# Hedgehog attention and squared-ReLU FFN: k's first tiles through the hardware queues, v's scaling in column pairs, q by whole rows

## Chip, cores and metric

The kernel runs on one core of a Trainium2 chip. The metric is the device time of one execution in microseconds; 11 executions of the kernel before were timed. A profiled execution has its own time, and a trace whose span begins with the first and ends with the last instruction.

## What is computed

```
phi(x)  = concat(exp(p), exp(-p)),  p = x @ w_phi - max|x @ w_phi|   # per row
kv      = phi(k)^T @ v              # per head: 256 x 64
z       = sum over rows of phi(k)
attn    = (phi(q) @ kv) / (phi(q) @ z + 1e-6)
x       = attn, heads side by side  # 4608 x 512
out     = relu(x @ w_in)^2 @ w_out  # 512 -> 2048 -> 512
```

q, k and v are 8 batches of 8 heads of 576 rows of 64, w_phi is 64 x 128, all fp32; the output is 4608 x 512, fp32. On chip the operands of all matmuls are bf16.

## The kernel before, in words

**Tiles.** A batch has 576 rows: 512 of each head go through tiles of 128 rows x 4, two heads (a pair) at a time, and the last 64 of each head, the short rows ("s", tile group 4), through tiles in which two heads lie one below the other. The FFN works on chunks of 512 rows: chunk c is the 512 long rows of batch c, and the ninth chunk holds the short rows of all batches (`xS`). The 8 batches' attention and the 9 chunks' FFN are interleaved, so that TensorE works on the FFN of one batch while VectorE and ScalarE prepare the next.

**A batch's attention.** k and q are loaded, transposed (`kT`, `qT`; on TensorE at line 616 for batches 0 and 1, by a transposing DMA on SP at line 626 for the others) and multiplied with w_phi (L642; for batch 0's k L670, for its q L816; q once more in the other orientation at L858). VectorE takes the maximum of the absolute values along a row (`mk` L722 and L677, `mq` L823). ScalarE takes exp of both signs (`kp`, `kn` L728 and L705; `qp`, `qn` L873). The maximum of k isn't subtracted ahead of exp: ScalarE turns it into the factors exp(-m) and exp(m) (L747; short rows L740), which stand in the 65th column of `va`, and VectorE multiplies v with them into the other 64 (L766; short rows L762). TensorE forms kv and z in one matmul of 65 columns (L783, L788), a copy brings it to `kv_sb`, and TensorE multiplies it with `qp` and `qn` (L888). VectorE scales the first part by `en` (L900), takes the reciprocal of the 65th column (L908) and multiplies (L912), which gives `xo`. Transposed (`xT`; L928 and L937 for batch 0, else by DMA), this is the FFN's input.

**A chunk's FFN.** 16 blocks of w_in (L1038; for chunk 0 in smaller pieces L1049), relu into `hr` on ScalarE or VectorE (L1015, L1017), the square into `h` on VectorE (L1024), w_out (L1103; the last tile L1067), a copy to `ot` (L441 or L439) and a store by SP.

**What sets the order.** Every step is entered in a plan as an operation with an engine, a cost, a key and what it reads and writes. A planner (`Machine.run`) runs through it with these costs, with the eight PSUM banks and with a model of the DMA queues, and writes the instructions of every engine in the order in which it picked them; `KEYS` are the sort keys of all operations, `RELEASES` are the earliest times of loads, and `STATES` tells for the operations that two engines can do (a plan's `either`) which one takes it. All of this is fixed when the kernel is built. Each engine then works through its list in order and waits by semaphores.

**Loads.** All loads but w_phi are issued by POOL (software queue), which casts fp32 to bf16 under way: per batch k and v in runs of 512-element pairs (`load`, L512), q in two halves of the columns of each row group (`load_q`, L532: 128 of 256 fp32 values of a row, 512 B), the short rows in two DMAs (L520). The first k pair is issued on its own. w_phi comes by the hardware queues of SP and ACT, a half each (L476). At most 8 software DMAs are under way: the ninth waits for the first.

**Fillers.** Where the plan has TensorE idle in the first 45 us, and a PSUM bank is free (`op.spare`), matmuls on a zero tile `warm` are inserted (L1195): at a cost of 0.11 us each up to 6 us, of 0.058 us after.

The scaling of v, before:

```
o = t[:, 8 * g0 : 8 * g1, :]
pin(nc.vector.tensor_tensor(
    out=o[:, :, :D], in0=xv[s2][:, 512 * g0 : 512 * g1].rearrange("p (m d) -> p m d", d=D),
    in1=o[:, :, D].to_broadcast([P, 8 * (g1 - g0), D]), op=ALU.mult))
```

## Time and profile before

| | |
|---|---|
| median of 11 executions | 362.6 us (361.89 to 363.67) |
| the profiled execution's own time | 362.73 us |
| its span in the trace | 360.8 us |
| TensorE matmuls, busy | 344.0 us (95% of the span) |
| VectorE, busy | 292.6 us (81%) |
| ScalarE, busy | 232.2 us (64%) |
| POOL, busy | 112.5 us (31%) |
| DMA | 39.62 MB in 102631 packets; 77248 of them under 512 B |

Busy time is the union of an engine's instructions; a matmul's end is modelled, so that TensorE counts as busy in short waits too. Slices are a fortieth of the span, 9.02 us each. In rows of groups the numbers after the count are busy us and mean ns of one instruction, then the idle time ahead of them and what ended it. GB/s are bytes as written, bf16 for the cast loads.

### The profile page before, as it was taken

How to read it: one execution, taken by the hardware profiler on the slowest of the kernel's cores; microseconds unless marked ns; L12 is line 12 of the kernel's file. 1: busy time of each engine (PE TensorE's matmuls, PEld its weight loads, DVE VectorE, ACT ScalarE, POOL GpSimd, SP SyncE). 2: the span in 40 equal slices, each digit the busy share in tenths (PEclk: the TensorE clock that was granted, in tenths of full speed). 3: DMA queues.
4: the chain of work that ended last, by engine and by line, in shares of the span. 5: the costliest groups of instructions: out<-in, count | busy, mean ns of one | idle time of the engine just before them, and what ended most of it. 6: DMA issues, size and time to landing. Idle time of an engine off the chain costs nothing.

```text
span 360.8 us, 8564 instructions
## 1 busy us (share of the span) xinstructions
PE 344.0 (95%) x3412; PEld 197.6 (55%) x3442; DVE 292.6 (81%) x503; ACT 232.2 (64%) x434; POOL 112.5 (31%) x167
## 2 busy tenths in 40 slices
PE   8669999999999999999999999999999999999995
PEld 7368886554554555446544555555455554444444
DVE  4998999789999977899789888999798965686131
ACT  3986899588888783959677847957785340310320
POOL 8636727356635951364405211020000000000000
PEclk9859999999999999999999999999999999999999
DMA  8999999997999999998957754448230031100213
GB/s 92 189 201 143 182 187 119 164 163 95 143 167 133 156 125 182 172 145 119 90 111 92 128 94 109 93 69 122 79 99 2 17 95 45 36 0 2 111 35 89
DMA packets 102631, 39.62 MB, mean 110 GB/s; under 512 B 77248, under 2 KB 98112, under 8 KB 102592
## 3 DMA queue, kind: packets, MB, share of 16 engines
q0 software_dynamic: 51744, 18.36, 48.7%
q1 hardware_dynamic: 50608, 20.55, 25.9%
q8 instruction: 27, 0.44, 0.5%
q10 hardware_dynamic: 240, 0.16, 0.2%
q14 instruction: 12, 0.10, 0.1%
HBM read 36.77 MB, written 9.44 MB: 128 GB/s over the span
## 4 chain that ended last, share of the span: by engine, by line
PE 64%; DVE 8%; ACT 7%; issue 2%; DMA 1%; DVEq 0%; ACTq 0%
PE psum L1103 27%; PE psum L1038 24%; PE psum L888 4%; DVE mq L823 3%; PE psum L642 3%; PE psum L783 3%; ACT kp L728 2%; PE psum L858 2%; DVE va L766 2%; ACT kn L728 2%; DMA xq<-in_q_dram 1%; DVE h L1024 1%; DVE mk L722 1%; PE psum L1067 1%; ACT va L740 1%
## 5 line engine op out<-in xcount | busy, mean ns | idle before, releaser
L1103 PE MATMUL psum<-wout,h 128*128 128x512 bf16 x530 | 127.4, 379 | 2.4 <-issue 1.3
L1038 PE MATMUL psum<-xT,win 128*128 128x512 bf16 x448 | 104.9, 379 | 0.6 <-ACT hr L1015 0.4
L1015 ACT ACTIVATE hr<-psum 128x512 bf16<-128x512 f32 x91 | 53.6, 598 | 49.7 <-PE psum L1038 28.2
L1103 PEld LDWEIGHTS <-h 128*128 128x128 bf16 x560 | 50.7, 98 | 56.8 <-issue 2.7
L1038 PEld LDWEIGHTS <-win 128*128 128x128 bf16 x512 | 47.5, 98 | 53.6 <-issue 1.7
L1024 DVE TENSOR_TENSOR h<-hr 128x512 bf16<-128x512 bf16 x144 | 56.8, 416 | 16.2 <-ACT hr L1015 15.3
L873 ACT ACTIVATE qp<-psum 128x1024 bf16<-128x1024 f32 (+1 forms) x40 | 37.3, 939 | 20.2 <-PE psum L858 17.7
L532 POOL DMA_DIRECT2D xq<-in_q_dram x52 | 37.7, 726 | 39.8 <-ACT hr L1015 9.5
L823 DVE TENSOR_REDUCE mq<-psum 128x8 f32<-128x1024 f32 (+1 forms) x40 | 43.7, 1109 | 4.6 <-PE psum L642 3.8
L1017 DVE TENSOR_SCALAR hr<-psum 128x512 bf16<-128x512 f32 x53 | 36.0, 682 | 9.8 <-PE psum L1038 8.3
L722 DVE TENSOR_REDUCE mk<-psum 128x8 f32<-128x1024 f32 (+1 forms) x35 | 38.1, 1107 | 2.4 <-PE psum L642 1.7
L728 ACT ACTIVATE kp<-psum 128x1024 bf16<-128x1024 f32 (+1 forms) x35 | 32.8, 938 | 10.2 <-DVE mk L722 10.2
L766 DVE TENSOR_TENSOR va<-xv,va 128x1024 bf16<-128x1024 bf16 (+1 forms) x36 | 38.6, 1099 | 0.6 <-ACT va L747 0.4
L873 ACT ACTIVATE qn<-psum 128x1024 bf16<-128x1024 f32 (+1 forms) x40 | 37.4, 940 | 2.0 <-PE psum L888 2.0
L900 DVE TENSOR_TENSOR psum<-psum,en 128x520 f32<-128x520 f32 (+1 forms) x40 | 27.9, 700 | 7.1 <-PE psum L888 6.1
L728 ACT ACTIVATE kn<-psum 128x1024 bf16<-128x1024 f32 (+1 forms) x35 | 32.9, 948 | 0.1
L912 DVE TENSOR_TENSOR xo<-psum,rden 128x512 bf16<-128x512 f32 (+1 forms) x40 | 27.3, 686 | 0.9
L512 POOL DMA_DIRECT2D xv<-in_v_dram x26 | 18.9, 727 | 28.1 <-ACT qp L873 10.5
L512 POOL DMA_DIRECT2D xk<-in_k_dram x28 | 20.2, 721 | 20.7 <-ACT va L747 7.5
L783 PE MATMUL psum<-va,kp 128*128 128x65 bf16 x256 | 20.9, 197 | 0.1
L441 ACT ACTIVATE ot<-psum 128x512 f32<-128x512 f32 x24 | 14.4, 603 | 10.0 <-PE psum L1103 6.8
L783 PE MATMUL psum<-va,kn 128*128 128x65 bf16 x256 | 20.6, 197 | 0.1
(68 smaller groups left out, 406.3 us busy)
## 6 DMA issues: line engine op xcount, KB each, us to landing
out_dram<-ot SPq DMA_DIRECT2D x32, 256.0 KB, 2.6
xk<-in_k_dram POOLq DMA_DIRECT2D x26, 128.0 KB, 4.0
xv<-in_v_dram POOLq DMA_DIRECT2D x24, 128.0 KB, 4.1
xq<-in_q_dram POOLq DMA_DIRECT2D x48, 64.0 KB, 3.5
win<-in_moe_w_in_dram POOLq DMA_DIRECT2D x4, 512.0 KB, 11.3
wout<-in_moe_w_out_dram POOLq DMA_DIRECT2D x4, 512.0 KB, 8.1
xq<-in_q_dram POOLq DMA_DIRECT2D x4, 256.0 KB, 8.0
xv<-in_v_dram POOLq DMA_DIRECT2D x2, 512.0 KB, 9.0
```

Of the source, the lines that this page charges most:

```text
L512: pin(nc.gpsimd.dma_start(out=x[:, a * 512 : z * 512].rearrange("p (h x) -> p h x", x=4 * D), in_=src[b][2 * a : 2 * z, 0:512, :].rearrang ...
L532: pin(nc.gpsimd.dma_start(out=x[:, jj * 1024 + a * 256 : jj * 1024 + z * 256].rearrange("p (h x) -> p h x", x=128), in_=q[b][2 * a : 2 * z ...
L722: pin(nc.vector.tensor_reduce(out=mk_view(g), in_=ps2(pj)[:, :, : n * Fd].rearrange("p e (i f) -> p e i f", f=Fd), axis=AX.X, op=ALU.max, ...
L728: pin(nc.scalar.activation(out=dst[slot][:, :, :n, :].rearrange("p e i f -> p e (i f)"), in_=ps2(pj)[:, :, : n * Fd], func=ACT.Exp, scale= ...
L766: pin(nc.vector.tensor_tensor(out=o[:, :, :D], in0=xv[s2][:, 512 * g0 : 512 * g1].rearrange("p (m d) -> p m d", d=D), in1=o[:, :, D].to_br ...
L783: pin(nc.tensor.matmul(out=o[:, sg, hi, :], lhsT=(kp, kn)[sg][kgroup[pr]][:, j % 2, 2 * hi + j // 2, :], rhs=va[s2][sg_of(sg, pr)][:, 8 * ...
L823: pin(nc.vector.tensor_reduce(out=mqb[:, c, :, :n], in_=ps2(pj)[:, :, : n * Fd].rearrange("p e (i f) -> p e i f", f=Fd), axis=AX.X, op=ALU ...
L873: pin(nc.scalar.activation(out=o, in_=i_, func=ACT.Exp, scale=sgn))
L1015: pin(nc.scalar.activation(out=hr[sl], in_=ps1(g), func=ACT.Relu))
L1024: pin(nc.vector.tensor_tensor(out=dst, in0=i_, in1=i_, op=ALU.mult))
L1038: pin(nc.tensor.matmul(out=o, lhsT=win[mc // 4][:, kc, mc % 4 * P : (mc % 4 + 1) * P], rhs=x, start=(kc == 0), stop=(kc == KC - 1)))
L1103: pin(nc.tensor.matmul(out=ps1(g), lhsT=h2[c % 2][mc // 4][:, mc % 4, tt * P : (tt + 1) * P], rhs=wout[mc // 4][:, mc % 4, :], start=(mc = ...
```

## The change

It has five parts and a new plan.

- **k's first tiles of batch 0** (pairs 0 and 1 and the short rows) no longer come by POOL. SP issues the two pieces of the short rows, pair 0 and half of w_phi, ACT issues pair 1 and the other half, all fp32, into the output tiles `ot`, which aren't used yet. Three copies on VectorE or ScalarE cast them to `xk`. w_phi's fp32 tile and the fillers' zero tile now lie in `otl`.
- **v is scaled in column pairs.** `va` has 66 columns instead of 65; the factor is written twice (by one ScalarE instruction whose input is read with step 0), and VectorE's operation reads it as pairs: innermost two adjacent elements with step 1, then 32 times the same pair. For the short rows one operation on 8 x 64 becomes two on 4 x 64.
- **q is loaded by whole rows**, as k and v are: per pair 256 fp32 values of a row, 1 KB; for batch 0 in two DMAs of four heads each. Which tile of `qT` belongs to which step changes with it: every second tile (`2 * h + c // 2`) where four adjacent ones were.
- **The square** of the FFN can be done by ScalarE (`ACT.Square`) too.
- **The planner** keeps PSUM bank 7 for the fillers up to 27 us of its time, and the slack that it adds to loads is smaller.
- `KEYS`, `STATES`, `RELEASES` and some limits are new. In the order that results, ScalarE does 72 of the 144 squares, VectorE 72 relus where 53 were, 20 kv copies where 9 were, and 17 output copies where 11 were. There are 191 fillers where 118 were, 30 of them ahead of the first transposes where 52 were. TensorE's other matmuls are the same in number and shape; POOL issues 26 DMAs fewer.

```diff
-SLACK = {"first": 1.2, "v0": 2.5, "ld": 0.8, "x": 1.2, "kq": 1.0}
+SLACK = {"first": 0.6, "v0": 1.0, "ld": 0.6, "x": 0.8, "kq": 1.0}
-WARM_UP, COLD = 45.0, 6.0
+WARM_UP, RESERVED, COLD = 45.0, 27.0, 6.0
...
-        self.free_at = [0.0] * self.BANKS
+        self.free_at = [0.0] * (self.BANKS - 1) + [RESERVED]
...
+            if name == "PE" and t < RESERVED:
+                spare = self.BANKS - 1
...
-    D1 = D + 1
+    D1, D2 = D + 1, D + 2
...
-    va = [[sb(f"va{b}{s}", [40, D1]) for s in range(2)] for b in range(2)]
+    va = [[sb(f"va{b}{s}", [40, D2]) for s in range(2)] for b in range(2)]
...
+    wphi_f = otl[:, 128 : 128 + Fd]
+    warm = otl[:, 256 : 256 + P // 2].bitcast(BF16)
...
+    kf = {0: ot[0], 1: ot[1], "s": ot[2]}
...
+    def first_k(g, name, e, lat):
+        def fn():
+            pin(e.dma_start(
+                out=kf[g].rearrange("p (h x) -> p h x", x=4 * D),
+                in_=k[0][2 * g : 2 * g + 2, 0:512, :].rearrange("h (p j) d -> p h (j d)", j=4)))
+        first_ops.append(add(name, (0.6, lat), -10, fn, w=[("ot", g)], what="xk"))
...
+    first_k(0, "SP", nc.sync, 2.9)
+    first_w(1, "ACT", nc.scalar)
+    first_w(0, "SP", nc.sync)
+    for hi in range(2):
+        first_s(hi, "SP", nc.sync, 3.0)
+    first_k(1, "ACT", nc.scalar, 3.6)
+
+    for n, g in enumerate((0, 1, "s")):
+        def fn(g=g):
+            if g == "s":
+                copy(xk[0][:, 2048:2304], kf[g][:, :256])
+            else:
+                copy(xk[0][:, g * 512 : g * 512 + 512], kf[g])
...
-    def load_q(b, key, jjs=(0, 1), single=True, release=0.0, prs=((0, 4),)):
...
-                        pin(nc.vector.tensor_tensor(
-                            out=o[:, :, :, :D], in0=x, in1=o[:, :, :, D].to_broadcast([P, 4, 2, D]), op=ALU.mult))
+                        for h in range(2):
+                            pin(nc.vector.tensor_tensor(
+                                out=o[:, :, h, :D].rearrange("p m (a t) -> p m a t", t=2),
+                                in0=x.rearrange("p m (a t) -> p m a t", t=2),
+                                in1=o[:, :, h, D:D2].to_broadcast([P, 4, 2, D // 2]).rearrange("p m t a -> p m a t"), op=ALU.mult))
...
                         pin(nc.vector.tensor_tensor(
-                            out=o[:, :, :D], in0=xv[s2][:, 512 * g0 : 512 * g1].rearrange("p (m d) -> p m d", d=D),
-                            in1=o[:, :, D].to_broadcast([P, 8 * (g1 - g0), D]), op=ALU.mult))
+                            out=o[:, :, :D].rearrange("p m (a t) -> p m a t", t=2),
+                            in0=xv[s2][:, 512 * g0 : 512 * g1].rearrange("p (m a t) -> p m a t", t=2, a=D // 2),
+                            in1=o[:, :, D:D2].to_broadcast([P, 8 * (g1 - g0), 2, D // 2]).rearrange("p m t a -> p m a t"),
+                            op=ALU.mult))
...
+            return [2 * h + c // 2 for h in (range(8) if first else range(c % 2 * 4, c % 2 * 4 + 4))]
...
+            if now[0].eng == "ACT":
+                pin(nc.scalar.activation(out=dst, in_=i_, func=ACT.Square))
+            else:
+                pin(nc.vector.tensor_tensor(out=dst, in0=i_, in1=i_, op=ALU.mult))
+        o = add("DVE", dve_cost(256), key, fn, r=[("hr", sl)], w=toks, what="sq")
+        plan.either((o, "ACT", act_cost(512)))
...
-    load(k, xk, 0, -8, "xk", prs=((1, 2), (2, 4)), single=False)
-    load_q(0, -7.5, jjs=(0,), single=False)
+    load(k, xk, 0, -8, "xk", prs=((2, 4),), single=False)
+    load(q, xq, 0, -7.5, "xq", prs=((0, 2), (2, 4)))
```

## The prediction, made before the result

> **What bounds the kernel now.** I read the page's slices first, then the busy times by window, then the timeline of the first 34 us, then the groups with shapes kept apart.
>
> ```profile
> PE   8669999999999999999999999999999999999995
> PEclk9859999999999999999999999999999999999999
> ```
>
> From the fourth slice (27 us) on, TensorE is busy nine tenths of the time at full clock, to the last slice. So the kernel is bound by TensorE, except for its beginning. The windows (window and its length, then busy us and count of PE, PEld, DVE, ACT and POOL, then clock, DMA share, GB/s) put sizes on it:
>
> ```profile
> 14.00:26.00 12.00, 6.29 (x79) 5.49 (x80) 11.69 (x22) 11.48 (x31) 5.45 (x8) 0.58 1.38 199
> 26.00:34.00 8.00, 8.00 (x159) 7.03 (x158) 7.33 (x17) 5.36 (x12) 4.45 (x7) 0.99 1.26 149
> 34.00:60.00 26.00, 25.04 (x439) 21.51 (x439) 25.51 (x48) 22.90 (x41) 16.84 (x24) 1.00 1.32 166
> 60.00:120.00 60.00, 58.22 (x604) 31.40 (x610) 54.91 (x85) 49.27 (x93) 31.29 (x47) 1.00 1.17 143
> 120.00:240.00 120.00, 118.77 (x1146) 63.09 (x1155) 105.03 (x174) 89.68 (x166) 40.96 (x60) 1.00 0.83 122
> 240.00:300.00 60.00, 59.24 (x569) 31.74 (x574) 51.68 (x91) 34.88 (x62) 2.72 (x4) 1.00 0.31 72
> ```
>
> From 14 to 26 us VectorE (11.69 of 12) and ScalarE (11.48) are full, while TensorE waits and its clock is at 0.58. From 34 us to 300 us TensorE's idle time is only 0.96 + 1.78 + 1.23 + 0.76 = 4.7 us. The timeline shows why the beginning is long:
>
> ```profile
> 6.13 0.38 PE L616 MATMUL psum<-ident,xk 128*128 128x128 bf16 x4
> ...
> 10.83 0.62 PE L616 MATMUL psum<-ident,xk 128*128 128x128 bf16 x8
> ...
> 14.52 0.27 PE L616 MATMUL psum<-ident,xk 128*128 128x128 bf16 x2 [0.63 <-DMA xk<-in_k_dram]
> ...
> 18.59 1.01 PE L616 MATMUL psum<-ident,xq 128*128 128x128 bf16 x8 [1.24 <-DVE mk L677]
> ...
> 33.15 1.06 PE L1049 MATMUL psum<-xT,win 128*128 128x128 bf16 x16
> ```
>
> The first pair of k is transposed at 6.13 us, the next at 10.83, the short rows at 14.52, and the first FFN matmul (L1049) starts at 33.15. All of batch 0's attention must lie ahead of it, and on VectorE these are large groups:
>
> ```profile
> L766 DVE TENSOR_TENSOR va<-xv,va 128x512 bf16<-128x512 bf16 x8 | 5.3, 684 | 0.1
> L762 DVE TENSOR_TENSOR va<-xv,va 128x512 bf16<-128x512 bf16 x2 | 1.3, 692 | 0.0
> ```
>
> **What the Trainium skill says.** "Vector Engine (DVE) Microarchitecture Reference", 5.1: two-source operations reach two elements a cycle when every operand is 16 bits with innermost step 1; one element read again and again as an operand ran at one. The trace agrees: L766 takes 684 ns for 512 elements and 1217 ns for 1024 (one a cycle), while the square L1024, all dense, takes 416 ns for 512. That a dense pair whose next dimension has step 0 still counts isn't shown by a run here. "TensorE: Matmul & The Clock Gate", Part 1: an idle window of about 3.4 us halves the clock. It agrees: 0.50 from 16 to 26 us in windows of 2 us, after gaps of 1.3 to 2.2 us with little work between. "DMA: Bandwidth & Descriptors", "Issuing engines are not separate DMA queues": hardware and software queues share the same 16 engines. The trace has too little hardware traffic in that stage to show it.
>
> **The change, part by part.** Counts are from the built order of both programs, durations from the trace.
>
> *k on the hardware queues, in fp32.* Two w_phi halves are issued on them at 0.74 us, take 0.58 us each to issue and land 2.1 to 2.5 us later. SP now issues two short k pieces, k's first pair and a half of w_phi; ACT k's second pair and the other half: 0.69 MB. At the 0.39 MB/us that 195 GB/s of bf16 written means in fp32 read, they take 1.8 us together, so the last lands at about 0.74 + 2.3 + 1.8 = 4.8 us. A cast to bf16 is added: the one of w_phi (128 wide) took 450 ns, a 512-wide one lies between that and 0.85 us; I take 0.65. k's first two pairs and short rows are then transposed at 4.3 to 5.6 us where they were at 6.1, 10.8 and 14.5. TensorE's program allows it: 30 filler matmuls stand ahead where 52 did; at 107 ns each while cold, 3.2 us from 0.99, so it is ready at 4.2.
>
> *TensorE's floor.* Ahead of the first FFN matmul stand, after the change, 66 transposes (56 ns), 72 projections of k and q (28), Fq 8 wide and 2 narrow (108 and 54), 64 + 8 for kv (29 and 57) and 48 for the output (30): 10.2 us. Before it was 9.9 (60 transposes, 40 output). There are 22 changes of row tiling where 16 were, at 0.1 us (254.13 to 254.44 us on the timeline: two L858 that need 0.22 take 0.31), and 189 fillers where 118 were. The fillers can't be skipped: 30 x 0.107 + 159 x 0.056 = 12.1 us. Floor: 1.0 + 10.2 + 2.2 + 12.1 = 25.5 us. Before, the same sum is 1.0 + 9.9 + 1.6 + 8.8 = 21.3, and the trace had 33.15: 11.9 us of waits and half clock. The fillers now have a PSUM bank of their own, so that the clock should stay up.
>
> *VectorE up to there.* Counting its new order up to the second xT copy: 3 casts 1.75, copies of kT and qT 1.96, maxima of k 0.83 + 8 x 0.68, v scaled 8 x 0.417 + 4 x 0.29, kv copies 0.84, maxima of q 4 x 1.21 + 0.68, output steps 2.1 + 0.4 + 0.7 + 0.6: 24.6 us of durations. In a queue each overlaps the next by about 0.08 (two of 0.68 take 1.28), 44 times: 21.1. Scaling v at two a cycle is what saves: 512 wide 0.684 to 0.417, 1024 wide 1.217 to 0.68 (0.53 less for 512 cycles less), and each L762 becomes two of 256, 0.29 each, 0.58 for 0.69. At the 97% of the window from 14 to 26, 21.1 becomes 21.8; from 4.8 it ends at 26.6. ScalarE's list up to there adds up to about the same, 20 us after overlap from 4.4, so it doesn't end later. I take the first FFN matmul at 27.0, that is 6.15 us earlier.
>
> *q by whole rows.* The same bytes in half the packets, 1 KB of fp32 instead of 512 B. The first q step now needs both halves of the heads instead of one half of the columns. The software ring writes 0.195 MB/us; v (0.59 MB), q's first heads, k's second half, a few short pieces and one w_in stand ahead of q's second half, 1.7 MB or 8.8 us; from 3.3 and with the hardware queue's 1.8 us, it lands near 14 to 15. TensorE's order comes to it at about 14.2. Cost nothing, up to 1 us if late. POOL issues 26 fewer DMAs at 0.72 us; it was 31% busy: nothing.
>
> *Edits with one answer.* The fp32 k lies in the output tiles `ot`, w_phi and the fillers' operand in `otl`: the first output copy waits for casts done tens of us before, nothing. Scale factors written twice (16 values instead of 8, 32 instead of 16) add 7 to 13 ns to rows of 271 ns; kv's operand rows one element farther apart and q's tiles read at every second place cost TensorE between nothing and, if each of the 64 wide Fq were to double, 64 x 0.108 = 6.9 us: nothing in the trace reads that way; I take nothing, since their width stays.
>
> *The rest, 33.15 to 360.8, 327.65 us.* 0.35 us of work is done earlier. Ten more tiling changes cost 0.9 (114 in all become 130). 72 of 144 squares go to ScalarE, 19 relus, 11 kv copies and 6 output copies to VectorE. By occupancy VectorE falls from 278 to 251 us and ScalarE rises from 210 to 231; neither is the bound. What this can return is TensorE's idle 4.7 us; half of the 2.7 before 120 us, where VectorE was 94% busy, and a quarter of the 2.0 after: 1.9. Rest: 327.65 - 0.35 + 0.9 - 1.9 = 326.3.
>
> Sum: 27.0 + 326.3 = 353.3 us of span. The profiled execution took 362.73 with a span of 360.8, 1.93 more; it is 0.13 above the median 362.6. 353.3 + 1.93 - 0.13 = **355.1**.
>
> **Rivals.** (1) *Transfers set the beginning.* Up to the last w_in tile the ring writes 4.2 MB: 21.4 us at 0.195, from 3.3 plus 1.8 for the hardware queue: 26.5, needed at about 29.5 (third FFN block). At 0.15 MB/us, near the 125 GB/s of the first 14 us, it is 33: 3.5 us late, 358.6. For it: DMA share above 1 all through. Against: 190 to 208 GB/s from 10 to 26 us. (2) *More is returned*: TensorE meets its floor of 25.5 and all of 4.7: 25.5 + 323.5 + 1.8 = 350.8. (3) *Slower, by ScalarE's queue.* It is in order; a square whose relu VectorE makes waits there, and behind it stand the exponentials and the relus that free TensorE's banks. From 34 to 120 us ScalarE is busy 72 of 86 us; in the first three batches about 14 squares come to it (7 us). It decides once its waits for VectorE in that stretch exceed the 7 us left; to undo the gain they must reach 14: 364.5. Against: TensorE has up to seven banks of slack for w_in's output. (4) *The column pairs don't run at two a cycle*: v costs what it did, plus two operations more for each short piece; 2.1 us at the beginning, and about half of 28 x 0.53 on a VectorE that is 90% busy, less what squares gave back: 359.5.
>
> **How the numbers follow.** Forecast (352.5 to 358) 0.55; (1) 0.17; (2) 0.13; (3) 0.08; (4) 0.07. About 0.2% is what a measurement of this kernel can tell from no change. Faster: 0.55 + 0.13 and most of (1) and (4), 0.86; within: 0.05; slower: 0.09. Range 350.5 (just below case 2) to 360.5 (first FFN matmul at 30.5, nothing returned: 30.5 + 328.2 + 1.8).
>
> **What would show it.** Right: k's transposes by 5.6 us; the first FFN matmul near 27; clock 1.0 from 10 us on; L805 at 0.42 and 0.68 us; one table load, as the built order has it. Wrong: v's scaling at 1.2 us; TensorE idle over 0.3 us on DMA before 30 us; ScalarE above 95% from 34 to 120 us; a first FFN matmul after 30.

## The result, and the profile after

The changed kernel takes 366.3 us (median of 12 executions, 365.46 to 368.25) where the kernel before takes 362.6: the ratio is 1.0101, with a 95% interval from 1.0087 to 1.0115. It is slower by 3.7 us, where 7.5 us less was forecast; the prediction was wrong in its sign. The profiled execution took 366.5 us with a span of 364.8, 4.0 more than before. All times within an execution, here and below, come from one profiled execution of each kernel, while executions of one kernel lie up to 2.8 us apart: differences of a few tenths between such times are not proven. Line numbers below are those of the changed kernel where its profile is read.

The windows, in the columns explained above the fence of the prediction, say in which stage the loss lies:

```profile
14.00:26.00 12.00, 11.87 (x202) 10.49 (x200) 7.99 (x19) 11.19 (x29) 6.00 (x9) 1.00 1.37 200
26.00:34.00 8.00, 7.78 (x119) 5.96 (x119) 6.62 (x10) 7.48 (x15) 2.25 (x3) 1.00 1.31 203
34.00:60.00 26.00, 25.64 (x417) 21.54 (x417) 25.04 (x53) 22.29 (x42) 10.79 (x16) 1.00 0.98 129
60.00:120.00 60.00, 58.28 (x660) 32.43 (x666) 52.70 (x91) 49.52 (x93) 26.02 (x40) 1.00 1.19 153
120.00:240.00 120.00, 118.37 (x1154) 62.70 (x1165) 96.74 (x167) 96.69 (x172) 34.97 (x52) 1.00 0.80 118
240.00:300.00 60.00, 59.69 (x553) 31.02 (x558) 49.09 (x87) 42.44 (x78) 1.40 (x2) 1.00 0.30 63
```

From 34 to 300 us TensorE is idle 0.36 + 1.72 + 1.63 + 0.31 = 4.0 us, against 4.7 before: no loss there. From 14 to 26 us VectorE has fallen from 11.69 to 7.99 us, ScalarE is as full as it was (11.19), and over half of TensorE's 11.87 is fillers (some 7 us). TensorE's timeline gives the size:

```profile
8.63 0.82 PE L640 MATMUL psum<-ident,xk 128*128 128x128 bf16 x6 [4.26 <-ACT xk L444]
...
12.39 4.14 PE L1236 MATMUL psum<-otl 128*128 128x128 bf16 x41
16.36 0.61 PE L640 MATMUL psum<-ident,xq 128*128 128x128 bf16 x8
17.59 0.61 PE L640 MATMUL psum<-ident,xk 128*128 128x128 bf16 x8
...
37.32 1.06 PE L1095 MATMUL psum<-xT,win 128*128 128x128 bf16 x16
```

k's first transposes start at 8.63 us (before: 6.13, forecast: 4.3), and the first FFN matmul at 37.32 (before: 33.15, forecast: 27.0). What follows it takes 364.8 - 37.3 = 327.5 us, where it took 327.65. So the whole loss, 4.2 us, lies ahead of the first FFN matmul, and the rest returned nothing. The DMA issues of the first 12 us (KB each, then median us from issue to landing) name the first cause:

```profile
ot<-in_k_dram ACTq DMA_DIRECT2D x1, 256.0 KB, 2.9
ot<-in_k_dram SPq DMA_DIRECT2D x1, 256.0 KB, 6.1
...
ot<-in_k_dram SPq DMA_DIRECT2D x2, 64.0 KB, 4.2
...
otl<-in_w_phi_dram ACTq DMA_DIRECT2D x1, 32.0 KB, 2.8
otl<-in_w_phi_dram SPq DMA_DIRECT2D x1, 32.0 KB, 6.4
```

ACT's pieces took 2.8 and 2.9 us, little more than w_phi did before (2.1 and 2.5), but SP's took up to 6.4. SP issued its half of w_phi at 2.87, so it landed at 9.3, where the forecast had the last piece at 4.8. The chain of work that ended last, followed back through the profile, begins with this DMA. The first steps of ScalarE, and then of VectorE:

```profile
6.87 1.28 ACT L444 ACT_TABLE_LOAD   x1 [6.87 <-DMA ot<-in_k_dram]
8.16 0.42 ACT L444 ACTIVATE xk<-ot 128x256 bf16<-128x256 f32 x1
...
10.11 0.38 ACT L741 ACTIVATE kp<-psum 128x256 bf16<-128x256 f32 x1 [0.67 <-PE psum L706]
```

```profile
3.67 0.43 DVE L442 CAST xk<-ot 128x512 bf16<-128x512 f32 x1 [1.53 <-DMA ot<-in_k_dram]
9.39 0.23 DVE L518 CAST wphi<-otl 128x128 bf16<-128x128 f32 x1 [5.30 <-DMA otl<-in_w_phi_dram]
9.54 0.42 DVE L442 CAST xk<-ot 128x512 bf16<-128x512 f32 x1
```

ScalarE's first instruction is now the cast of the short rows, and the table load (1.28 us, at 1.35 before) stands behind the wait for them. VectorE waits for w_phi until 9.39; only then can TensorE project anything, and the first exponential comes at 10.11, where it came at 7.53. Three things were as forecast: v's scaling runs as fast as forecast (the line's minimum, median and maximum in ns, below: 411 for 512, 681 for 1024), there is one table load, and the clock is at 1.00 from 14 to 300 us.

```profile
L805 DVE TENSOR_TENSOR va<-xv,va x36: 411/681/693, 17.7 to 285.4; 128x1024 bf16<-128x1024 bf16 x28, 128x512 bf16<-128x512 bf16 x8
```

### The profile page after: what moved, and what is told of

Same layout as the page of the kernel before. It is cut to its first block, busy times and chain, and to the rows that moved or that the text cites. A ratio compares the mean times of both kernels' runs of the same rounds, so it can differ in the third digit from the quotient of the medians.

```text
span 364.8 us, 8686 instructions
## 1 busy us (share of the span) xinstructions
PE 351.0 (96%) x3482; PEld 200.5 (55%) x3515; DVE 267.1 (73%) x481; ACT 256.8 (70%) x475; POOL 91.9 (25%) x138
## 4 chain that ended last, share of the span: by engine, by line
PE 82%; ACT 12%; DMA 2%; issue 2%; DVE 1%; SPq 1%; DVEq 0%; ACTq 0%
PE psum L1149 32%; PE psum L1084 26%; PE psum L930 5%; PE psum L678 4%; PE psum L1095 4%; PE psum L825 3%; PE psum L900 2%; PE psum L1236 2%; DMA otl<-in_w_phi_dram 2%; ACT hr L1057 2%; ACT h L1067 2%; ACT kp L764 1%; ACT qn L915 1%; ACT qp L915 1%; ACT kn L764 1%
## 5 line engine op out<-in xcount | busy, mean ns | idle before, releaser
L1149 PE MATMUL psum<-wout,h 128*128 128x512 bf16 x527 | 128.7, 379 | 2.6 <-issue 1.0
L1059 DVE TENSOR_SCALAR hr<-psum 128x512 bf16<-128x512 f32 x72 | 48.8, 684 | 22.4 <-PE psum L1084 16.4
L1057 ACT ACTIVATE hr<-psum 128x512 bf16<-128x512 f32 x72 | 42.5, 600 | 23.0 <-PE psum L1084 14.2
L1067 ACT ACTIVATE h<-hr 128x512 bf16<-128x512 bf16 x72 | 44.5, 632 | 13.6 <-DVE hr L1059 12.8
L915 ACT ACTIVATE qp<-psum 128x1024 bf16<-128x1024 f32 (+1 forms) x40 | 37.2, 943 | 11.4 <-PE psum L900 10.3
L915 ACT ACTIVATE qn<-psum 128x1024 bf16<-128x1024 f32 (+1 forms) x40 | 37.3, 947 | 2.0 <-PE psum L930 2.0
L1069 DVE TENSOR_TENSOR h<-hr 128x512 bf16<-128x512 bf16 x72 | 29.3, 418 | 12.8 <-ACT hr L1057 12.2
L942 DVE TENSOR_TENSOR psum<-psum,en 128x520 f32<-128x520 f32 (+1 forms) x40 | 27.6, 700 | 11.5 <-PE psum L930 11.4
L550 POOL DMA_DIRECT2D xq<-in_q_dram x27 | 19.5, 733 | 46.5 <-ACT hr L1057 12.5
L444 ACT ACTIVATE ot<-psum 128x512 f32<-128x512 f32 x18 | 10.7, 594 | 21.6 <-PE psum L1149 21.6
L805 DVE TENSOR_TENSOR va<-xv,va 128x1024 bf16<-128x1024 bf16 (+1 forms) x36 | 21.6, 624 | 2.8 <-ACT va L783 2.7
L550 POOL DMA_DIRECT2D xk<-in_k_dram x26 | 18.7, 724 | 18.7 <-ACT h L1067 7.4
L442 DVE COPY ot<-psum 128x512 f32<-128x512 f32 x17 | 11.7, 686 | 14.9 <-PE psum L1149 14.8
```

Of the source, the lines that this page charges most:

```text
L550: pin(nc.gpsimd.dma_start(out=x[:, a * 512 : z * 512].rearrange("p (h x) -> p h x", x=4 * D), in_=src[b][2 * a : 2 * z, 0:512, :].rearrang ...
L915: pin(nc.scalar.activation(out=o, in_=i_, func=ACT.Exp, scale=sgn))
L942: pin(nc.vector.tensor_tensor(out=o, in0=o, in1=enb[:m, c, :].rearrange("t (b h) -> t b h", b=2).to_broadcast([m, 2, 4, D1]), op=ALU.mult))
L1057: pin(nc.scalar.activation(out=hr[sl], in_=ps1(g), func=ACT.Relu))
L1059: pin(nc.vector.tensor_scalar(out=hr[sl], in0=ps1(g), scalar1=0.0, scalar2=None, op0=ALU.max))
L1067: pin(nc.scalar.activation(out=dst, in_=i_, func=ACT.Square))
```

## The experiments

Three theories. A: SP's pieces land late, because they follow each other in one queue and share the DMA engines with POOL's loads; the beginning follows its first landing. B: ScalarE's longer list bounds the beginning; ahead of the first FFN matmul it makes 8 copies of kT and qT of 512 columns where it made 3. C: the fillers, in a fixed order, hold ready work back. There are no numbers 5 and 15. Ratios are to the kernel before, run beside it.

**1, the table load first.** Behind ACT's two DMA issues:

```diff
+        if op.what == "wphi" and op.eng == "ACT":
+            pin(nc.scalar.activation(out=rden[2][:, :1], in_=warm[:, :1], func=ACT.Copy))
```

> The kernel after with one addition: a one-column ScalarE activation right after ACT's two DMA issues, so that the load of the activation table (1.28 us) no longer stands behind the short rows' DMA. Theory A (k is late because of the late pieces and of the table load behind them): the short rows' cast begins at 6.9 instead of 8.16 us, k's first transposes move from 8.63 to 7.4, the first FFN matmul from 37.3 to about 36.1, and the run takes 365.1. Theory B (ScalarE's longer list bounds the beginning): its list also starts 1.3 us earlier, but the exponentials wait for TensorE; the first FFN matmul gains 0.5 to 1.3 too, so this run alone doesn't part A from B. Theory C (the fillers hold the ready work back): they are a fixed number behind the transposes and shift along, 0.5 to 1.3.

Measured: 366.9 us, 1.0118 (1.0089 to 1.0148), no gain. The transposes moved from 8.63 to 7.48 as expected, the first exponential didn't (10.29): VectorE's cast of w_phi stood at 9.57. The table load was covered by a later landing.

**2, no software traffic beside the first pieces.** POOL's loads go behind, and wait for, VectorE's cast of k's first pair (`last_k`).

```diff
+    early = [o for n, o in enumerate(order) if o.eng == "POOL" and o.what != "ident" and (o.at < 4.1 or n < order.index(last_k))]
...
+    order[at:at] = early
+    early[0].gate = last_k
```

> The kernel after, but POOL's first loads (v, q's first heads, k's second half) are issued only after VectorE has cast k's first pair, so that no software traffic runs while the hardware queues bring k and w_phi. A diagnosis, not a remedy, since v and q come later. Theory A, as far as it blames the sharing of the DMA engines: SP's pieces (short rows, k's first pair, w_phi's half) all land by about 5 us instead of 6.8 to 9.3, and k's first transposes come at about 6.5 (the table load still lies behind the short rows). If SP's pieces land as late as before, the sharing is not what delays them. Time: v and q come 4 us later, so the run takes 366 to 369 under any theory.

The landings of the same DMAs:

```profile
ot<-in_k_dram SPq DMA_DIRECT2D x1, 256.0 KB, 3.5
...
ot<-in_k_dram SPq DMA_DIRECT2D x2, 64.0 KB, 3.3
...
otl<-in_w_phi_dram SPq DMA_DIRECT2D x1, 32.0 KB, 3.0
```

6.1, 4.2 and 6.4 us became 3.5, 3.3 and 3.0: with POOL silent, w_phi lands at 5.9 instead of 9.3. That POOL's loads (v, q's first heads, k's second half) delay SP's pieces is shown. The Trainium skill's "DMA: Bandwidth & Descriptors", "Issuing engines are not separate DMA queues", says that all issuers' DMAs run on the same 16 engines; the prediction cited it and used it in one direction only: it let the hardware queues' 1.8 us delay POOL's loads, and POOL's loads delay nothing. The run takes 366.1 us, 1.0097 (1.0068 to 1.0126): the first exponential came at 8.37, 1.7 earlier, and v, now later, took it back (VectorE waited 2.0 us for it; first FFN matmul at 36.92).

**3, the pieces spread evenly over both queues.**

```diff
-    first_w(0, "SP", nc.sync)
+    first_w(0, "SP", nc.scalar)
-        first_s(hi, "SP", nc.sync, 3.0)
+        first_s(hi, "SP", (nc.sync, nc.scalar)[hi], 3.0)
```

> The kernel after with the second short piece and SP's half of w_phi moved to ACT's hardware queue: SP issues one short piece and k's first pair, ACT issues k's second pair, a short piece and w_phi's halves. Theory A, as far as it blames SP's queue of four pieces: the short rows land near 4.5 us and k's first pair near 6 instead of 8.3, the first transposes come at 6.5 and the run takes 364 to 365. If it is only the sharing of the DMA engines with v's load, the bytes are the same and the last piece lands as late as before (about 9 us), now w_phi's; the run is within 0.7 us of 366.3. Theory B: no change in the time, since ScalarE's list isn't shorter.

Measured: 367.2 us, 1.0124 (1.0091 to 1.0158); first exponential at 10.40. The second short piece took 5.5 us and the halves of w_phi 6.4: the last bytes land as late from either queue. SP's queue as such is not the cause.

**10, w_phi ahead of k, the table load first.**

```diff
+    first = sorted((o for o in order if o.what in ("warm", "wphi") and o.eng != "PE"), key=lambda o: o.what)
+    order = first + [o for o in order if o not in first]
...
+        if op.what == "xk" and op.eng == "ACT":
+            pin(nc.scalar.activation(out=rden[2][:, :1], in_=warm[:, :1], func=ACT.Copy))
```

> The kernel after with all its hardware-queue loads kept, but w_phi's halves issued first on both queues, and the activation table loaded ahead of the first wait (a one-column activation, as in the first experiment). So far: taking the table load away alone moved k's transposes by 1.15 us and the exponentials not at all, since VectorE's cast of w_phi (its last half is the last piece of SP's queue, landed at 9.5) came later. Theory A (the last landing among the pieces starts everything, and the rest follows it in a fixed order): w_phi lands near 3 us, the short rows at 7 as they did, k's first pair near 9; the exponentials of the short rows begin at 8.0 to 8.5 instead of 10.1, the first FFN matmul comes at 35.0 to 36.3, the run takes 364.0 to 365.3. If the later pieces of k hold the chain, 365.5 to 366.3.

Measured: 366.8 us, 1.0107 (1.0082 to 1.0132); a miss. w_phi landed in 2.1 and 2.4 us, and the delay moved on to the pieces behind it:

```profile
ot<-in_k_dram ACTq DMA_DIRECT2D x1, 256.0 KB, 5.8
ot<-in_k_dram SPq DMA_DIRECT2D x1, 256.0 KB, 7.5
ot<-in_k_dram SPq DMA_DIRECT2D x2, 64.0 KB, 4.9
```

The short rows were cast at 9.02, k's first pair at 10.23; first exponential at 10.82. In all three orders (after, 3 and 10) the last of the 0.69 MB lands at 9.3 to 10.2 us.

**8, k by POOL again,** straight into `xk` and ahead of v; no casts, w_phi alone on the hardware queues, and POOL builds the identity ahead of them; all else as after.

```diff
-    first_k(0, "SP", nc.sync, 2.9)
+    first_k(0, "SP", nc.gpsimd, 2.9)
...
-        first_s(hi, "SP", nc.sync, 3.0)
+        first_s(hi, "SP", nc.gpsimd, 3.0)
-    first_k(1, "ACT", nc.scalar, 3.6)
+    first_k(1, "ACT", nc.gpsimd, 3.6)
...
+    order = first + early + [o for o in order if o not in first + early]
```

> The kernel after with its first part undone: k's first pairs and short rows come by POOL's software queue as bf16, ahead of v, without casts; w_phi's halves are alone on the hardware queues; the order of the other steps is left as it is. The short rows should land near 6.6 us, w_phi near 3, k's transposes begin at 6.7 and the exponentials at 8, 2 us earlier than after; v lands 2 to 3 us later. Theory A: the first FFN matmul comes at 35.3, the run takes 364 to 365. Theory B: ScalarE's list still takes what it takes; 0.2 to 0.8 us less, 365.5 to 366.1.

Measured: 364.7 us, 1.0066 (1.0046 to 1.0087), against 1.0101. ScalarE's and TensorE's timeline:

```profile
1.35 1.28 ACT L444 ACT_TABLE_LOAD   x1 [1.35 <-PEq L1412]
...
7.70 0.38 ACT L741 ACTIVATE kp<-psum 128x256 bf16<-128x256 f32 x1 [0.52 <-PE psum L706]
```

```profile
34.56 1.05 PE L1095 MATMUL psum<-xT,win 128*128 128x128 bf16 x16
```

The first exponential moved by 2.4 us and the first FFN matmul by 2.8, with ScalarE's list unchanged but for one cast: theory A in its wide form. Of the 4.2 us ahead of the first FFN matmul, this undoes 2.8; 1.4 stay. Of the time it gives back less, 1.3 us of 3.7 by the ratios, and the two intervals just touch.

**12, the short rows ahead of k's pairs in POOL's issues.**

```diff
-    early.sort(key=lambda o: {"xk": 0, "xks": 1}[o.what])
+    early.sort(key=lambda o: {"xk": 1, "xks": 0}[o.what])
```

> The kernel of the eighth experiment (k by POOL) with POOL's issues of k turned round: the two short pieces, which TensorE's order wants first, go ahead of k's two pairs. They land near 4.8 instead of 6.2 us; k's first pair lands near 6. Theory A in its wide form (the whole beginning follows its first landing, microsecond by microsecond): exponentials at 6.3 to 7.0 instead of 7.7, first FFN matmul at 33.2 to 33.9 instead of 34.6, run 363.3 to 364.0. If v's or q's landing or an engine holds it by then, 364.5 to 364.9.

Measured: 366.8 us, 1.0107 (1.0087 to 1.0126), slower than 8, with intervals that touch. The exponentials began 0.6 us earlier (7.08), but VectorE then waited 2.21 us for v and TensorE 0.58 for q; first FFN matmul at 34.88, 0.3 later than in 8. So the order gains nothing there, as v's and q's landings are late next; the rest of the 2 us isn't located (the profiled execution, at 366.0, was 0.8 faster than the median).

**4, without the fillers behind the first 30.**

```diff
-            while op.spare is not None and idle + (0.11 if idle < COLD else 0.058) < op.at - 0.03:
+            while op.spare is not None and op.at < 5.0 and idle + (0.11 if idle < COLD else 0.058) < op.at - 0.03:
```

> The kernel after without the 161 fillers behind the first 30. Theory C (fillers in a fixed order hold ready work back): q's first transposes come when q has landed, at 12.6 instead of 16.4 us, and the first FFN matmul moves from 37.3 to 34 or 35, the run takes 363 to 364. Theories A and B: TensorE isn't what ends last, so it only waits where it ran fillers; the clock is at half as it was, the first FFN matmul comes at 36.5 to 38.5, the run takes 365.5 to 367.5.

Measured: 369.4 us, 1.0169 (1.0115 to 1.0222). q's transposes came at 12.77 instead of 16.36, and the first FFN matmul at 37.78, later all the same; the clock was 1.00 from 14 to 26 us, 0.96 to 34 and 0.95 to 60. Theory C alone falls. By the medians the fillers are worth some 3 us, of four executions that spread from 367.6 to 371.3 (the profiled one is the slowest).

**17, half of the fillers from 5 to 20 us,** on the kernel of 11 (below):

```diff
-            for _ in range(n):
+            for _ in range(n // 2 if 5.0 < op.at < 20.0 else n):
```

> The kernel of the eleventh experiment (k by POOL, batch 0's copies by VectorE; first FFN matmul at 34.2, 364.8 us) with half of the fillers that the plan has between 5 and 20 us (about 50 less, 2.9 us of TensorE). There ScalarE waited 2.04 us for TensorE's kv matmul, which stood behind fillers that ran back to back from 8.9 to 12.7 and 14.5 to 15.3 us. If the fillers hold it: first FFN matmul at 32.7 to 33.5, run 363.3 to 364.1. If not (q and v land when they land, or the clock falls with fewer fillers): 34.0 to 35.5 and 364.6 to 366.

Measured: 364.35 us, 1.0051 (1.0031 to 1.0071), against 1.0054 for 11. TensorE now waited 1.56 us for q itself, its clock fell to 0.86 from 14 to 26, and the first FFN matmul came at 35.30, in an execution 1.1 us slower than the median. No gain in the time is visible; the fillers hid a wait for q.

**7 and 11, ScalarE's copies made by VectorE:** in 7 all of kT and qT in the beginning, on the kernel after; in 11 the six of batch 0, on the kernel of 8.

```diff
+moved = [o for w in ("Cxk", "Cxq") for o in sorted((o for o in order if o.what == w), key=lambda o: o.seq)[:5]]
...
+        if op in moved:
+            op.eng = "DVE"
```

> The kernel after, but the copies of kT and qT out of PSUM that ScalarE has in the beginning (5 of kT and 3 of qT of 512 columns, some narrower, of batches 0 and 1; about 5 us in all) are made by VectorE, at the same places of the order. Theory B (ScalarE's longer list bounds the beginning): the first FFN matmul comes 2 to 4 us earlier than 37.3, the run takes 362.5 to 364.5. Theory A (late landings alone): k's first exponentials come at 10.1 as they did, and with them everything: 365.7 to 366.5.

> The kernel of the eighth experiment (k by POOL; first FFN matmul at 34.6, 364.7 us) with the six copies of batch 0's kT and qT that ScalarE had now made by VectorE (3 us of ScalarE's list; batch 1's stay where they were, so that nothing new stands ahead of batch 0's output steps on VectorE). In that kernel ScalarE was busy 11.96 of 12 us from 14 to 26. Theory B: the first FFN matmul comes at 32.5 to 33.6, the run takes 362.7 to 363.8. If the beginning is one chain through all three engines in a fixed order, in which a step costs the same on either engine: 34.2 to 35.0 and 364.4 to 365.2.

Measured: 7 takes 368.7 us, 1.0156 (1.0119 to 1.0193), and its first FFN matmul comes at 38.90, 1.6 later: in its trace four of batch 1's copies stand between batch 0's output steps on VectorE. 11 takes 364.8 us, 1.0054 (1.0034 to 1.0074), with the first FFN matmul at 34.23, 0.3 earlier for 2.3 us less on ScalarE; its time can't be told from that of 8. Its waits from 7 to 35 us (total, times, longest), ScalarE's and VectorE's, show where the rest went:

```profile
...
ACT kv L444 <- PE psum L830: 2.0, 1, 2.0
ACT qp L915 <- PE psum L930: 0.8, 1, 0.8
ACT kT L444 <- PE psum L640: 0.6, 2, 0.3
```

```profile
DVE va L799 <- DMA xv<-in_v_dram: 1.5, 1, 1.5
DVE mq L865 <- PE psum L858: 1.3, 2, 0.7
```

**16 and 19, ScalarE's copies cut short.** Each of ScalarE's copies ahead of the first FFN matmul copies 64 columns (`copy(view[:, :1, :64], i_[:, :1, :64])`), on the kernel of 8; the tiles are cleared before. These runs leave most of the copies out.

> The kernel of the eighth experiment (k by POOL; first FFN matmul at 34.6), but each copy of kT or qT that ScalarE makes in the beginning (11, of batches 0 and 1) copies only 64 columns; the rest of those tiles is set to zero beforehand, while VectorE is idle. So the kernel leaves out most of these copies: ScalarE has some 3.5 us less to do, and nobody has more. If ScalarE's load bounds the beginning: first FFN matmul at 31.5 to 32.5, run 361.7 to 362.7. If the fixed order, with fillers and landings in it, holds it: 34.0 to 34.6 and 364.2 to 364.8.

> The kernel of the eighth experiment (k by POOL; first exponential at 7.7, first FFN matmul at 34.6, 364.7 us) with ScalarE's ten copies of kT and qT ahead of the first FFN matmul cut to 64 columns each, so most of these copies are left out; the tiles are cleared beforehand in idle time of VectorE and ScalarE. ScalarE has some 3.2 us less to do in the stretch, nobody has more. If ScalarE's load bounds it: first FFN matmul at 31.4 to 32.4, run 361.6 to 362.6. If the fixed order with the landings of v and q in it bounds it (the run in which VectorE took over six of these copies gained 0.3 us): 33.9 to 34.6 and 364.0 to 364.8.

Measured: 16 takes 364.9 us, 1.0063 (1.0047 to 1.0078); the clearing, 1.2 us a tile on VectorE, delayed k's first copies by 1 us, so it tells little. 19 takes 364.3 us, 1.0037 (1.0019 to 1.0055), and its first FFN matmul comes at 33.82: 0.7 us earlier than in 8 for 2.8 us less on ScalarE, with VectorE's load as it was; the intervals of 8 and 19 overlap. Theory B falls as the bound: by these two executions ScalarE's load is worth a quarter of itself, and the rest turns into waits.

**6 and 9, the column pairs alone, and their absence.** 6 is the kernel before with v in column pairs; 9 is the kernel after with

```diff
-                            out=o[:, :, :D].rearrange("p m (a t) -> p m a t", t=2),
-                            in0=xv[s2][:, 512 * g0 : 512 * g1].rearrange("p (m a t) -> p m a t", t=2, a=D // 2),
-                            in1=o[:, :, D:D2].to_broadcast([P, 8 * (g1 - g0), 2, D // 2]).rearrange("p m t a -> p m a t"),
+                            out=o[:, :, :D], in0=xv[s2][:, 512 * g0 : 512 * g1].rearrange("p (m d) -> p m d", d=D),
+                            in1=o[:, :, D].to_broadcast([P, 8 * (g1 - g0), D]),
```

that is, with v's long rows scaled as before; the short rows stay in pairs.

> The kernel before with one part of the change alone: v scaled in column pairs (the factor written twice, VectorE's operation in pairs, two operations for the short rows), nothing else moved. Before its first FFN matmul VectorE was full (11.69 of 12 us from 14 to 26) and had 10 rows of 0.68 us there. If VectorE bounds that beginning, 8 x 0.27 less leaves 1.5 to 2 us: first FFN matmul at 31.2 to 31.7, run 360.6 to 361.1. If ScalarE, as full (11.48 of 12), bounds it as well, it is 362.0 to 362.6. The later part: nothing, TensorE bounds it.

> The kernel after with v's long rows scaled as before, with one factor per column group read again and again (0.68 us for 512 columns instead of 0.42, 1.22 for 1024 instead of 0.68). Theory B: VectorE is idle 4 of the 12 us from 14 to 26, so 8 x 0.27 = 2.1 us there cost only where ScalarE's exponentials wait for it, 0 to 1 us; the later part gives VectorE 10 us more of work in 267 and costs nothing as long as TensorE bounds it: 366.3 to 367.5. If VectorE's relief does return something in the later part, as the prediction had it (1.9 us), the run is slower by that much more: 368 to 369.

Measured: 6 takes 361.9 us, 0.9973 (0.9959 to 0.9988), faster than both kernels. But its first FFN matmul is at 33.10, unmoved, although VectorE is busy 9.54 us from 14 to 26 instead of 11.69; the gain is in the rest (326.5 us instead of 327.65). 9 takes 379.4 us, 1.0456 (1.0417 to 1.0495), a miss by over 10: its rest takes 340.4 us, 12.9 more than after, for 28 x 0.53 = 15 us more on a VectorE that is busy 75%. What TensorE waited for from 60 to 300 us, first after, then in 9 (its L824 is after's L825):

```profile
...
PE psum L1084 <- DMA xT<-xo: 0.4, 1, 0.4
PE psum L900 <- ACT qn L915: 0.3, 1, 0.3
PE psum L930 <- ACT qp L915: 0.3, 1, 0.3
...
```

```profile
PE psum L824 <- DVE va L805: 2.7, 5, 0.6
PE psum L1083 <- DMA xT<-xo: 1.4, 1, 1.4
PE psum L678 <- DVE mq L864: 1.4, 2, 0.7
PE psum L824 <- DVE kv L442: 1.0, 1, 1.0
...
```

The new order has spent v's relief: it gave VectorE 19 relus, 11 kv copies and 6 output copies, and left v's scaling little slack. The beginning again doesn't follow VectorE: in 9 it has 1.9 us more to do there, and the first FFN matmul comes at 37.24, as after.

**13, 14 and 18, an earlier k in the old order,** all on the kernel of 6: in 13 POOL issues k's first pair ahead of v's short piece, in 14 that pair alone comes by the hardware queues behind w_phi, 0.26 MB, and 18 is 14 with the identity built first on POOL. Of the 52 fillers ahead of the first transposes, 42, 34 and 29 stay. From 14:

```diff
+        for h, e in enumerate((nc.sync, nc.scalar)):
+            pin(e.dma_start(out=ot[0][:, h * 256 : h * 256 + 256],
+                            in_=k[0][2 + h, 0:512, :].rearrange("(p j) d -> p (j d)", j=4)))
...
+        pin(nc.vector.tensor_copy(out=xk[0][:, 512:1024], in_=ot[0]))
```

> The kernel before with v in column pairs (the sixth experiment: 361.9 us, first FFN matmul at 33.1), and k's first pair issued by POOL ahead of v's first short piece instead of behind it; of the 52 fillers ahead of the first transposes 42 stay, so that they don't hold them. The pair lands 0.7 us earlier. If the beginning follows its first landing: first transposes at 5.5 instead of 6.3, first FFN matmul at 32.3 to 32.6, run 361.1 to 361.4. If q's second half or the short rows of k (TensorE waited 0.82 and 1.34 us for them at 14 and 18 us) hold it by then: first FFN matmul at 33.0, run 361.7 to 362.1.

> The kernel before with v in column pairs, and k's first pair alone by the hardware queues in fp32, a head on each, behind w_phi's halves, with a cast on VectorE; 34 of the 52 fillers ahead of the first transposes stay. This is the idea of the change with 0.26 MB instead of 0.69 on the hardware queues, and with w_phi ahead. If it lands before the software queue's traffic fills the DMA engines (near 4 us): transposes at 4.7, 1.6 us earlier, and all of POOL's loads are issued 0.7 us earlier too; a beginning that follows its first landing gives a first FFN matmul at 31.5 to 32.0, run 360.3 to 360.9. If it is slowed as in the kernel after: lands at 6 to 8, first FFN matmul at 33.5 to 35, run 362.3 to 363.8. If later landings hold the chain: 361.5 to 362.1.

> The kernel of the fourteenth experiment (the kernel before, v in column pairs, k's first pair alone by the hardware queues; 360.6 us, first FFN matmul at 33.0), with the identity matrix built by POOL ahead of its first DMA issue, which costs every later issue about 0.3 us less or more, and 29 fillers ahead of the first transposes instead of 34. The transposes come at 4.9 instead of 5.4. If the beginning follows its first step: first FFN matmul at 32.4 to 32.6, run 360.0 to 360.2. If landings of k's short rows and q's second half, which POOL issues at the same times as it did, hold it: first FFN matmul at 32.9 to 33.1, run 360.4 to 360.8.

Measured: 361.1 us, 0.995 (0.9932 to 0.9968); 360.6 us, 0.9943 (0.9925 to 0.9962); 360.9 us, 0.995 (0.9936 to 0.9965). All three beat both kernels; their intervals separate them neither from each other nor clearly from 6. In 13 the time is as expected, but by luck: the transposes came at 6.13, not at 5.5, since they waited for the identity (0.47 us), and the first FFN matmul at 33.48. In 14 the halves of k's pair landed in 2.4 and 3.0 us:

```profile
ot<-in_k_dram ACTq DMA_DIRECT2D x1, 128.0 KB, 3.0
ot<-in_k_dram SPq DMA_DIRECT2D x1, 128.0 KB, 2.4
```

```profile
5.41 0.58 PE L616 MATMUL psum<-ident,xk 128*128 128x128 bf16 x4 [0.60 <-POOL ident L1133]
```

So k in fp32 by the hardware queues isn't slow in itself: little over a third of the bytes, behind w_phi and landed while the software queue's large loads were just beginning, arrives at 4.4. The transposes then waited for the identity, and 18 took that wait away (4.93); yet the first FFN matmul came at 32.97 and 34.28 (in an execution 1.4 us slower than 18's median) against 33.10 in 6. An earlier first step gains nothing visible there in the old order. The gain of 14 over 6, 1.1 us by the ratios, isn't clear of noise, and most of it isn't located.

## Why the prediction was wrong, point by point

The forecast of the span was 353.3 us, the trace has 364.8. Of these 11.5 us, 10.3 lie ahead of the first FFN matmul and 1.2 behind it. The table holds what the traces give, in us; the stretch runs from the first exponential to the first FFN matmul, and busy times are those in it.

| kernel | first exponential | first FFN matmul | stretch | ScalarE busy | VectorE busy | rest |
|---|---|---|---|---|---|---|
| before | 7.53 | 33.15 | 25.6 | 21.9 | 23.5 | 327.65 |
| after | 10.11 | 37.32 | 27.2 | 25.1 | 20.7 | 327.5 |
| 6, before with pairs | 7.68 | 33.10 | 25.4 | 21.7 | 21.4 | 326.5 |
| 8, k by POOL | 7.70 | 34.56 | 26.9 | 25.1 | 20.6 | 328.0 |
| 11, six copies to VectorE | 7.40 | 34.23 | 26.8 | 22.8 | 21.7 | 328.0 |
| 19, copies cut short | 7.71 | 33.82 | 26.1 | 22.3 | 20.6 | 328.6 |

**"They take 1.8 us together, so the last lands at about 0.74 + 2.3 + 1.8 = 4.8 us": the first failed step.** The last landed at 9.3. The step divided the hardware queues' bytes by the whole rate of the DMA engines, while the paragraph on q had v's 0.59 MB on the same engines from nearly the same moment; that paragraph let the hardware queues' bytes delay POOL's, and nobody let POOL's delay these. It also took no account of which piece each engine's first instruction waits for. Its size: VectorE's list was to start at 4.8 and started at 9.39, 4.6 us. Experiment 2 shows the sharing, 3 and 10 that no order within the pieces mends it, and 8 that undoing it gives back 2.8 of the 4.2 us lost ahead of the first FFN matmul.

**"At the 97% of the window from 14 to 26, 21.1 becomes 21.8": the second.** The sum of VectorE's list was right (21.4 us busy from 9.39 to the first FFN matmul, for 21.1). That the stretch would be as long as the list was not: from 9.39 it took 27.9 us, 5.7 more than 21.8 and the 0.4 to the first matmul. The window showed VectorE full, and I read from it that VectorE bounds the beginning. Experiment 6 shows that it did not in the kernel before either: 2.1 us less in that window moved the first FFN matmul by 0.05. VectorE's waits of over 0.2 us after 10 us, in the kernel after, are these (total, times, longest):

```profile
...
DVE mk L713 <- ACT kn L741: 2.3, 2, 1.3
DVE va L805 <- ACT va L783: 1.7, 2, 1.4
DVE mq L865 <- PE psum L858: 1.4, 2, 0.7
DVE psum L942 <- PE psum L930: 0.6, 1, 0.6
DVE mk L713 <- PE psum L706: 0.3, 1, 0.3
```

4.0 us are waits for ScalarE and 2.3 for TensorE.

**"ScalarE's list up to there adds up to about the same, 20 us … so it doesn't end later": the third, a mis-sized term.** It is busy 25.1 us in the stretch, 3.2 more than before; the five added copies of kT and qT of 512 columns (0.5 us each) are most of that. But 11 and 19 show that this load alone isn't the bound either: 2.3 and 2.8 us less gave 0.3 and 0.7. The chain of work that ended last, in the kernel after, passes through the fillers and then through ScalarE:

```profile
2.87 6.43 DMA otl<-in_w_phi_dram
...
12.46 4.07 PE psum L1236 x41
...
16.79 0.60 ACT qT L444
...
28.77 0.92 ACT qn L915
```

So fewer fillers (4) or a lighter ScalarE (11, 19) can each be hidden by the other. 17 lessens both and gained nothing visible, but with a lower clock and a wait for q, so that it doesn't settle this. What is shown is that the stretch stays between 26 and 28.6 us in the new order whichever engine is relieved, and shifts with its first landing until v and q are late; what makes the new order's stretch 1.3 us longer than the old one's (26.9 in 8, 25.6 before) stays open. Of it, 19 accounts for 0.7. No run has the new order, or q by whole rows, without the other parts.

**"The fillers can't be skipped."** They were counted as a floor of 12.1 us. After leaving them out TensorE wasn't earlier (4), so the floor never bound. (The counts and prices that went into it add up to 10.4 us of work ahead of the first FFN matmul, not 10.2.) That they keep the clock up was right: from 14 to 26 us it is 0.86 in 17 and 1.00 in 11; in 4 it fell only after 26. How long an idle time halves the clock stays open: before, it was at half from 16 to 26 us, while TensorE's longest idle time was 0.6 us between 1 and 15.7 us and 2.2 up to 26, so that the 3.4 us that the prediction names are not what this trace shows.

**"What this can return … 1.9", and "Ten more tiling changes cost 0.9".** For each matmul from the first of the FFN on I took the time to the next one's start and subtracted its cost by shape (216 ns for 512 columns, 56 for 128, and so on; up to 0.11 for a change of tiling). The changes grew from 100 to 108 and from 10.3 to 11.1 us: right. Work and losses need care, since some matmuls have no record: of the program's 560 products with w_out of 512 columns, 530 are in the trace before and 527 in the one after, and the 6.5 and 7.1 us of the others look like losses. With them put back, work fell by 0.2, as it is done earlier (0.35 was forecast), and TensorE's losses are 7.2 us before and 6.6 after: 0.6 returned, instead of 1.9. In 6 they are 6.1, so the pairs return 1.1 in the old order; in 9 they are 19.5. The relief was real, and the new order spent about all of it.

**The rivals.** None was it. The second expected more gain. The first blamed transfers, but w_in's, at the end of the beginning; the third had the sign and the engine, but it was to decide once ScalarE's squares wait over 7 us for VectorE from 34 to 120 us: they waited 1.4, and ScalarE is busy 71.8 us of 86 there, as before (72.2). The fourth is refuted by L805; had it held, the price was 4.4 us in the prediction and would have been nearer 13 by experiment 9. A range that ended at 360.5 left no room for a k that comes later than before; the case "the pieces moved are slower than those they replace" wasn't among them, although the part of the trace it needs was said to be missing ("The trace has too little hardware traffic in that stage to show it"). An unknown of that kind belongs in the range from both sides.

## What to carry to other kernels

Moving a load to another queue moves its issue, not its bytes: before giving it a landing time, list what every other queue has on the same DMA engines in those microseconds, and find the last piece that the first instruction of each engine waits for. A small, early piece that is done before the big loads start landed at 4.4 us and cost nothing; nearly three times as much lost 2.6 us at the first exponential, and with the smallest and most needed piece first (10) no less. A full engine in a window is not yet the bound: relieve it by a known amount first, as one edit alone, and see whether the next milestone moves; and what an edit is worth depends on the order planned around it (the column pairs gained 1.0 us in the old order; taking them out of the new one, which was planned with them, cost 13).

## What the runs showed of the hardware that was not expected

- A hardware-queue DMA of 32 KB took 2.1 to 3.0 us from issue to landing with the software queue silent or hardly begun, and 6.4 beside POOL's loads (512 KB of v first); 256 KB took 2.8 to 3.5 and 5.7 to 7.5.
- A two-source VectorE operation whose second operand is a dense pair repeated with step 0 runs as fast as an all-dense one, which the prediction had assumed without a run: 411 ns for 512 elements, 681 for 1024 (the square of 512 takes 418).
- A cast from fp32 to bf16 of 512 columns on VectorE took 0.42 or 0.43 us in 15 of 18 cases (0.68 at most), where the prediction took 0.65.
- The activation table is loaded ahead of the first activation, but not always behind its wait: at 6.87 us after and 5.27 in 2, behind the wait for the short rows' DMA, and at 1.35 before and in 8, whose first activation then waited for TensorE until 7.53 and 6.80. An activation of one column moved it to 1.78 (1). What decides isn't shown.
